# Reload of x split around the turned Wp pieces, and one load of normalised rows moved behind the last turn of q

## The chip, the core and the metric

The kernel runs on one core of one Trainium2 chip. Its engines are TensorE (matmuls, PE in the profile; its weight loads are PEld), VectorE (DVE), ScalarE (ACT), GpSimd (POOL) and SyncE (SP, which here only issues DMAs). Each engine works through its own instructions in their order, and semaphores let one wait for another. DMAs are issued by SP, ScalarE and GpSimd and run on the core's 16 DMA engines; a DMA that the code calls `dma_start_transpose` turns 2-byte blocks on the way. The metric is the device time of one execution in microseconds (us).

## The reference

Forward and backward pass of one transformer block, B=1, S=2048 rows, D=640, H=32 heads of 20, F=1728, all in bfloat16.

```python
h  = x + attn(layernorm(x), wqkv, wo)      # linear attention:
#   q, k, v = heads of x @ wqkv;  phi(t) = where(t > 0, t + 1, exp(t)) + 1e-6
#   kv = phi(k)^T v;  z = sum(phi(k));  o = phi(q) kv / (phi(q) z + 1e-6);  attn = o @ wo
h2 = h + (silu(n @ w1) * (n @ w3)) @ w2    # n = layernorm(h)
# outputs: h2, and the gradients of x, wqkv, wo, w1, w3 and w2 for a given grad_out
```

## The kernel before

The order of all work is written out by hand: within an engine the instructions stand in the order in which the Python code issues them, and tile pools and semaphores are derived from that. Rows of x come in 16 tiles of 128; `x_sb` holds them in on-chip memory, normalised in place. TensorE does nearly all the work and goes through these stages:

- 0 to 73 us: layernorm of x, the k part and a few q tiles (`q_tile`), and the product of phi(k) with the normalised x (`m_part(m, tiles)`, line L430, five blocks m of 128 columns, each over all 16 row tiles). `m_part(4, ...)` is the last reader of the normalised x: it runs in three calls, over tiles 0 to 4, 5 to 10 and 11 to 15. While it runs, finished q tiles are divided by their denominators (`r_row`) and turned into `pqT` by a DMA (`r_T(t)`, L385).
- 73 to 98 us: the remaining q tiles (`q_late`), the folded matrix Wp (`f2_wT(i)`, i from 0 to 4: matmuls L705, copies on ScalarE and VectorE L708, and a turning DMA per 128 columns, L709), and the first attention outputs `f2_half(t, j)` (`f2_at`, matmuls L657; j is the half of 320 columns). They are added to the rows of the raw x, so x has been loaded again into `x_sb` by then: `load_x(a, b)`, L187, loads tiles a to b-1. For tiles 0 to 3 with j=0 and for tile 4 VectorE adds x (L664), for the others of the first eight TensorE does it with an identity matmul (L655). Between them stand single `mlp_ghh(n)` steps (L395, tile `mm`), which read 128 columns each of the turned second weight, `w2T` (`load_w2T(a, b)`, L457); columns 4*128 to 8*128 belong to n = 4 to 7.
- 98 to 340 us: the gated MLP; then to 398 us the gradient of w2, and to 535 us the backward pass through the MLP's layernorm and the attention output (`ghn`, `gr`).
- 535 to 561 us: `q_parts()` (L1219, tile `gwo`), a generator of 20 steps; it makes q's gradient-side products in five blocks m of 128 columns. When a block is done ScalarE copies it to `qp` (L1222), and SP turns it into `QT` (L1226; both are parts of the tile `tri`). `part(n)` runs the next n steps, and the loads of the stage are issued between them: `load_xnT(c)` (L1242) loads and turns 512 normalised rows, `load_wqT(k)` (L1299) loads and turns 640 rows of wqkv.
- 561 to 612 us: four half jobs of the q gradient (`fill(4)`, tile `job`), then `gkvT` (L1388), five blocks whose fourth and fifth read the last block of QT, then small squares, and from 580 us a loop over the 16 row tiles that uses `xnT` (L1441, tile `dkv`, three buffers). In each round VectorE adds `gzb` into `gp` (L1444) and multiplies with `pkb` (L1445), which `load_pk` (L1410) loads by pairs of tiles.
- 612 to 699 us: the gradient of x (`gxn`), and from 699 us the gradients of w1 and w3 (`grad_job`, tile `job`, eight accumulators, 16 matmuls each): ScalarE copies each finished job to a slot of `obs` and issues its stores.

On SP's queue the stretch of the first part of the change reads, in order: r_T(0), r_T(1), a turn of m, r_T(2), `load_w2T(4P, 8P)`, r_T(3), `load_x(0, 6)`, the five Wp pieces, r_T(4), r_T(5). The stretch of the second part reads: turn of QT block 0, `load_xnT(1)`, blocks 1, 2 and 3, `load_xnT(2)`, block 4, `load_xnT(3)`, `load_wqT(0)`, the load of m (`mN`), the store of `dwoT`, four loads of pk.

The DMAs that SP and ScalarE issue take eight semaphores in turn; each waits until the one that last used its semaphore, eight before it, has landed.

Of the kernel before, what the change touches and what calls it, by code (L numbers as in the profile page):

```python
# [9 lines left out]
P = 128  # L10
# [10 lines left out]
ST, DT = S // P, D // P  # L21
# [34 lines left out]
def kernel(  # L56
# [74 lines left out]
    class Stats:  # L131
# [13 lines left out]
        def part(self, src, t, j, mid=None):  # L145
            if j == 0:
                self.st[t] = cp.tile([P, 2, 6], F32, name="st6", bufs=4)
            V.bn_stats(out=self.st[t][:, j, :], in_=src[:, t, j * HD:(j + 1) * HD])
            if j == 0:
                return  # L150
            V.bn_aggr(out=self.mv[:, t, :], in_=self.st.pop(t)[:])
            if mid is not None:
                mid()
            V.tensor_scalar(out=self.ve[:, t:t + 1], in0=self.mv[:, t, 1:2], scalar1=EPS_LN, scalar2=None, op0=ALU.add)
            G.tensor_tensor(out=self.rs[:, t:t + 1], in0=self.ve[:, t:t + 1], in1=mhalf[:, 0:1], op=ALU.pow)
# [30 lines left out]
    def load_x(a, b):  # L186
        dma(out=x_sb[:, a:b, :], in_=xS[:, a:b, :])  # L187
# [86 lines left out]
    def p1_mm(t, n0, between=None, halves=None):  # L274
        acc = p1_acc() if halves is None else None
        for j in range(2):
            p1_half(acc[:, j, 0:HD] if halves is None else halves[j][:, 0:HD], t, n0 + j * HD)
            if j == 0 and between is not None:
                between()
        return acc  # L280
# [9 lines left out]
    def phi(acc, dst, t, parts=None):  # L290

        mq, rq = parts or phi_tiles()
        if parts is None:
            kw = dict(scale=ln1.rs[:, t:t + 1]) if t < RAW else {}
            A.activation(two(mq[:]), acc[:, :, 0:HD], AF.Exp, **kw)
            A.activation(two(rq[:]), acc[:, :, 0:HD], AF.Relu, **kw)

        def rest():
            V.tensor_scalar(out=mq[:], in0=mq[:], scalar1=1.0, scalar2=1e-6, op0=ALU.min, op1=ALU.add)
            V.tensor_tensor(out=dst, in0=mq[:], in1=rq[:], op=ALU.add)  # L300
        held.append(rest)
# [9 lines left out]
    def q_home(t):  # L311
        if t < 4 or 8 <= t < 10:
            pqs[t] = pq6[:, t if t < 4 else t - 4, :]
        elif t < 8:
            pqs[t] = pf.tile([P, D], BF16, name="pql", bufs=4)[:]
        else:
            pqs[t] = pkx[0][:, DT + t - 10, :]
# [3 lines left out]
    def q_tile(t):  # L321
        q_home(t)
        phi(p1_mm(t, 0), pqs[t], t)
# [35 lines left out]
    def r_prod(t):  # L359
        for j in range(2):  # L360
            js = slice(j * HD, (j + 1) * HD)
            if t < 8:
                pr[t, j] = (p1.tile([P, HD], F32, name="pr", bufs=2) if t % 2 else
                            pf.tile([P, HD], F32, name="pr", tag="h2", bufs=2))[:]
            else:
                pr[t, j] = ps.tile([P, 512], F32, name="prp", tag="at", bufs=2)[:, 0:HD]
            (G if t < 8 else V).tensor_tensor(out=pr[t, j], in0=pqs[t][:, js], in1=Zb[:, js], op=ALU.mult)
# [16 lines left out]
    def r_T(t):  # L384
        dmaT(out=pqT[:, :, t * P:(t + 1) * P], in_=pqs[t])  # L385
# [39 lines left out]
    def m_part(m, tiles, js=(0, 1)):  # L425
        if m not in macc:
            macc[m] = [ps.tile([P, 512], F32, name="macc", tag=("m", "tr")[m % 2], bufs=2) for _ in range(2)]
        for t, j in [(t, j) for t in tiles for j in js]:
            n = HD + (m < 2) * j
            T.matmul(macc[m][j][:, 0:n], lhsT=pk_all[:, t, m * P:(m + 1) * P],  # L430
                     rhs=x_ext[:, t, j * HD:j * HD + n], start=(t == 0), stop=(t == ST - 1))
# [12 lines left out]
    def kvT_block(m, acc):  # L444

        a, b = M_H[m]
        n = (b - a) * DH
        for c in range(DT):
            T.matmul(acc[:, 0:n], lhsT=wqkv[:, c, 2 * D + m * P:2 * D + (m + 1) * P],
                     rhs=mT[:, c, a * DH:b * DH], start=(c == 0), stop=(c == DT - 1))  # L450
        masked(bd, acc[:, 0:n], m)
# [4 lines left out]
    def load_w2T(a, b):  # L456
        dmaT(out=w2T[:, :, a:b], in_=B_w2[a:b, :])  # L457
# [116 lines left out]
    def big():  # L574
        return ps.tile([P, 2, 512], F32, name="bigx", tag="big", bufs=2)[:, 0]
# [45 lines left out]
    m_part(3, range(11, ST))  # L621
    m_end(3)
    r_T(2)
    load_w2T(4 * P, 8 * P)
    dmaG(out=m_v[:, 1:4, :], in_=mbs[:, 1:4, :])
    r_head(3)
    r_prod(5)
    m_part(4, range(5))
    q_tile(8)
    kvT_block(1, big())  # L630
    r_row(4)
# [6 lines left out]
        m_part(4, range(11, ST), (j,))  # L638
        m_end(4, (j,))
    ps.release()  # L640
    load_x(0, 6)


    ps = pool("pap", space=PSUM)
# [56 lines left out]
    def f2_wT(i):  # L701

        acc = [ps.tile([P, 512], F32, name="wt", tag=("o2", "at")[i % 2], bufs=2) for _ in range(2)]
        for c, a, b, bank, off, first in SQ:
            T.matmul(acc[bank][:, off:off + (b - a) * DH], lhsT=wo[:, c, i * P:(i + 1) * P],  # L705
                     rhs=bd[:, c, a * DH:b * DH], start=first, stop=True, skip_group_check=True)
        for bank, (a, b) in enumerate(((0, SPLIT_D), (SPLIT_D, H))):
            (A.copy, V.tensor_copy)[bank](out=pkx[0][:, i, a * DH:b * DH], in_=acc[bank][:, 0:(b - a) * DH])  # L708
        dmaT(out=Wp[:, :, i * P:(i + 1) * P], in_=pkx[0][:, i, :])  # L709
# [234 lines left out]
    def kv3():  # L944
# [2 lines left out]

    run((q_late, 10, f2_mT), (q_late, 11, kv3), (phi_rest,),
        (q_late, 12, lambda: (f2_wT(0), f2_wT(1))), (q_late, 13, lambda: (f2_wT(2), f2_wT(3))),
        (f2_wT, 4), (phi_rest,), (q_late, 14), (r_T, 4), (r_head, 5), (r_prod, 7),  # L950
        (q_out, 10, 14), (mlp_ghh, 4),
        (q_late, 15), (w2_room,), (sig_table,), (f2_half, 0, 0), (f2_half, 1, 0), (f2_half, 2, 0), (f2_half, 3, 0), (mlp_ghh, 5),
        (f2_half, 0, 1), (r_store, 4, 5), (f2_half, 1, 1), (f2_hn, 0), (r_store, 5, 6), (f2_half, 2, 1), (f2_hn, 1),
# [42 lines left out]
    for c in range(SC):  # L996
# [9 lines left out]
        for fc in range(FT):  # L1006
# [8 lines left out]
            if c == 0 and fc in (5, 7, 9, 11):  # L1015
                a, b = {5: (0, 3), 7: (3, 6), 9: (6, 10), 11: (10, 13)}[fc]
# [13 lines left out]
            if c == SC - 1 and fc in (1, 2, 5, 6):  # L1030
                i = (1, 2, 5, 6).index(fc)
# [48 lines left out]
    for n in range(len(blk) * DT):  # L1080
        b, m = divmod(n, DT)
# [155 lines left out]
    def load_xnT(c):  # L1237

        if c % 2 == 0:
            both = ba.tile([P, 2, DT, W], BF16, name="xnT", tag="ggb", bufs=2)  # L1240
            xnT[c], xnT[c + 1] = both[:, 0], both[:, 1]
        dmaT(out=xnT[c], in_=xn_d[c * W:(c + 1) * W, :])  # L1242
# [48 lines left out]
    a, b = ST - 1, ST - 2  # L1291
# [20 lines left out]
    load_xnT(1)  # L1312
    part(4)
    part(4)
    load_xnT(2)
    part(20)
    V.reduce_sum(out=gz[:], in_=gz8[:], axis=AX.X)


# [5 lines left out]
    def grad_job(lhs, m, rhs, n, out, q=dma):  # L1325
        for _ in grad_halves(lhs, m, rhs, n, out, q):
            pass
# [107 lines left out]
    for t in range(ST):  # L1435
        c, i = divmod(t, TPC)
# [38 lines left out]
    def load_block(i, a=0, b=NB):  # L1475
        if i < len(blocks):
            f0, f1 = blocks[i]
            if a == 0:
                gb[i] = ex.tile([P, ST, NB], BF16, name="gb", bufs=2)
            b = min(b, f1 - f0)  # L1480
            dmaT(out=gb[i][:, :, a:b], in_=gg_d[f0 + a:f0 + b, :])

    def both_grads(m, f0, f1):

        return [(max(f0, lo) - f0, min(f1, lo + F) - f0, out[:, m, max(f0, lo) - lo:min(f1, lo + F) - lo])
                for lo, out in ((0, out4S), (F, out5S)) if max(f0, lo) < min(f1, lo + F)]
# [57 lines left out]
    def gw2_turn(b):  # L1544
        n = (blk[b][1] + P - 1) // P
        dmaT(out=g_h[:, turned[b]:turned[b] + n, :], in_=gw2T_d[:, b * 512:b * 512 + n * P])

    def gw2_out(b):
        f0, fw = blk[b]
        n, k = fw // P, turned[b]  # L1550
        dma(out=out_6[f0:f0 + n * P, :].rearrange("(k p) d -> p k d", p=P), in_=g_h[:, k:k + n, :])
        if fw % P:
            dma(out=out_6[f0 + n * P:f0 + fw, :], in_=g_h[0:fw % P, k + n, :])

    for i, (f0, f1) in enumerate(blocks):
        n = f1 - f0
        for m in range(DT):
            last = (i, m) == (len(blocks) - 1, DT - 1)
            for a, b in ((0, n - P), (n - P, n)) if last else ((0, n),):
                c = (a + b) // 2  # L1560
                halves = ((a, c), (c, b)) if i * DT + m < 7 else ((a, b),)
                out = [(x + y - a, z + y - a, to) for y, w in halves for x, z, to in both_grads(m, f0 + y, f0 + w)]
                grad_job(hnN, m, lambda t: gb[i][:, t, a:b], b - a, out, A.dma_start)
        load_block(i + 2)
        if 0 < i <= 4:
            gw2_out(i - 1)
        if i < 4:
            gw2_turn(i)
# [36 lines left out]
```

## Time and profile before

| | |
|---|---|
| median of 3 runs | 819.78 us (819.46 to 819.90) |
| the profiled execution | 820.36 us, of which 818.6 us lie between its first and last instruction (its span) |
| TensorE clock granted | 1.000 |
| instructions | 13711 |
| read from and written to HBM | 47.09 MB and 53.43 MB |

Times in the profile count from the first instruction. A line of a timeline gives start, duration, engine, source line, operation, what it writes and reads, shape, how many instructions are merged into it, and in brackets how long the engine was idle before and what ended that. An engine with a q behind its name (SPq) is its sequencer, which issues DMAs; the duration there is that of the issue, and the transfer lands later. A line of waits gives the waiting line, what released it, the total in us, how often, and the longest.

### The profile page before, as it was taken

The numbers are of one execution on the slowest core, as the hardware profiler recorded it, in microseconds if no ns is written. First come the engines' busy times: TensorE is split into PE (matmuls) and PEld (weight loads), VectorE is DVE, ScalarE is ACT, GpSimd is POOL, SyncE is SP. The second block draws the span as 40 slices with busy tenths as digits, with TensorE's granted clock in tenths as the row PEclk, the third lists the DMA queues.
The fourth block names the chain that finished last, engine by engine and source line by source line (L and its number), as shares of the span: only waits on it lengthen the run. The fifth ranks groups of instructions, "written<-read, shape, count | busy, mean of one in ns | idle before, by whom it ended". The sixth has DMA issues, their size and how long they took to land.

```text
span 818.6 us, 13711 instructions
## 1 busy us (share of the span) xinstructions
PE 811.6 (99%) x5261; PEld 501.6 (61%) x5292; DVE 452.7 (55%) x973; ACT 324.8 (40%) x609; POOL 131.7 (16%) x198
## 2 busy tenths in 40 slices
PE   9999999999999999999999999999999999999998
PEld 6777544555555555754577777777777777544444
DVE  7859997998898566300057777772781544200000
ACT  7856688665565666011112212222212334211111
POOL 2243333323222212100001111110220000000000
PEclk9999999999999999999999999999999999999999
DMA  9899899696485556999877877269994888979991
GB/s 262 207 242 277 206 276 302 207 244 174 128 209 158 169 168 168 239 254 243 233 178 181 218 194 193 58 111 181 269 217 93 179 193 153 249 175 235 221 239 37
DMA packets 335889, 162.46 MB, mean 198 GB/s; under 512 B 252560, under 2 KB 329072, under 8 KB 335824
## 3 DMA queue, kind: packets, MB, share of 16 engines
q1 hardware_dynamic: 291920, 120.68, 63.8%
q0 software_dynamic: 7328, 24.48, 8.9%
q10 hardware_dynamic: 36576, 16.42, 8.2%
q8 instruction: 41, 0.67, 0.3%
q14 instruction: 24, 0.20, 0.1%
HBM read 47.09 MB, written 53.43 MB: 123 GB/s over the span
## 4 chain that ended last, share of the span: by engine, by line
PE 96%; DMA 1%; ACT 1%; DVE 1%; issue 0%; SPq 0%; POOL 0%; DVEq 0%
PE mm L395 20%; PE job L1335 19%; PE ghn L1131 14%; PE gxn L1504 8%; PE gw L1086 7%; PE big L268 4%; PE o L913 4%; PE o L859 3%; PE gwo L1219 3%; PE macc L430 3%; PE gr L1188 3%; PE dkv L1441 3%; PE at L657 2%; DMA wqkv<-in_A_wqkv_dram 1%; PE dkv L1369 1%; DMA tri<-tri 1%
## 5 line engine op out<-in xcount | busy, mean ns | idle before, releaser
L1335 PE MATMUL job<-gb,hnN 128*128 128x496 bf16 (+3 forms) x576 | 116.8, 366 | 0.0
L1131 PEld LDWEIGHTS <-ggb 128*128 128x128 bf16 x864 | 84.5, 98 | 33.0
L395 PE MATMUL mm<-pqT,w 128*128 128x512 bf16 x396 | 93.2, 379 | 0.5
L1335 PEld LDWEIGHTS <-hnN 128*128 128x128 bf16 x576 | 55.8, 98 | 61.0
L395 PEld LDWEIGHTS <-w 128*128 128x128 bf16 x540 | 52.6, 98 | 62.9 <-issue 0.6
L1339 ACT CAST obs<-job 128x496 bf16<-128x496 f32 (+4 forms) x56 | 28.5, 510 | 123.6 <-PE job L1335 123.6
L1131 PE MATMUL ghn<-w13a,ggb 128*128 128x320 bf16 x448 | 63.5, 299 | 0.0
L1146 DVE SCALAR_TENSOR_TENSOR wb<-gs,hnb 128x640 f32<-128x640 bf16 x16 | 13.2, 825 | 88.1 <-ACT gs L1143 88.1
L1131 PE MATMUL ghn<-w13b,ggb 128*128 128x320 bf16 x416 | 61.4, 299 | 0.0
L395 PE MATMUL mm<-g2T,w2T 128*128 128x512 bf16 x228 | 58.8, 379 | 0.6
L1086 PE MATMUL gw<-hb,g 128*128 128x512 bf16 (+2 forms) x316 | 58.4, 345 | 0.2
L1086 PEld LDWEIGHTS <-g 128*128 128x128 bf16 x320 | 31.3, 98 | 27.0
L420 ACT CAST ghh<-mm 128x512 bf16<-128x512 f32 x48 | 28.2, 588 | 48.2 <-PE mm L395 41.4
L1196 POOL TENSOR_TENSOR sz<-Zb,g_h 128x640 f32<-128x640 bf16 x16 | 20.2, 1262 | 163.7 <-DVE g_h L1197 163.7
L796 ACT ACTIVATE sig<-mm 128x512 bf16<-128x512 f32 x56 | 33.7, 602 | 25.0 <-PE mm L395 21.6
L1143 ACT ACTIVATE gs<-ghn 128x640 bf16<-128x640 f32 x16 | 11.3, 705 | 76.0 <-PE ghn L1131 76.0
L395 PEld LDWEIGHTS <-w2T 128*128 128x128 bf16 x260 | 25.4, 98 | 23.4
L268 PEld LDWEIGHTS <-pqT 128*128 128x128 bf16 x320 | 30.7, 98 | 13.5 <-ACT pqT L260 0.9
L268 PE MATMUL big<-wqkv,pqT 128*128 128x320 bf16 x250 | 38.4, 299 | 0.2
L1335 PEld LDWEIGHTS <-g 128*128 128x128 bf16 x320 | 31.0, 98 | 11.5
L832 DVE TENSOR_TENSOR gate<-gate,sig 128x1024 bf16<-128x1024 bf16 x28 | 19.3, 689 | 33.9 <-ACT gate L807 31.1
L1091 ACT CAST gw2o<-gw 128x512 bf16<-128x512 f32 (+2 forms) x20 | 10.4, 519 | 66.6 <-PE gw L1086 25.3
(217 smaller groups left out, 1391.2 us busy)
## 6 DMA issues: line engine op xcount, KB each, us to landing
hh_d<-hhT SPq DMA_DIRECT2D x24, 256.0 KB, 2.8
gg_d<-gate POOLq DMA_DIRECT2D x24, 256.0 KB, 4.4
gg_d<-ghh POOLq DMA_DIRECT2D x24, 256.0 KB, 4.1
ggb<-gg_d SPq DMA_DIRECT2D x6, 896.0 KB, 5.3
ggb<-gg_d ACTq DMA_DIRECT2D x6, 832.0 KB, 5.7
ggb<-gg_d SPq DMA_DIRECT2D x2, 1728.0 KB, 13.9
pk_d<-pk_all SPq DMA_DIRECT2D x4, 640.0 KB, 5.4
g<-in_grad_out_dram SPq DMA_DIRECT2D x4, 640.0 KB, 5.7
```

Source lines behind the costliest of these rows:

```text
L268: T.matmul(acc, lhsT=pqT[:, c, t * P:(t + 1) * P], rhs=wqkv[:, c, n0:n0 + HD], start=(c == 0), stop=(c == DT - 1))
L395: T.matmul(acc[:], lhsT=w[:, c, fc * P:(fc + 1) * P], rhs=rhs[:, c, :], start=(c == 0), stop=(c == DT - 1))
L420: A.copy(out=ghh[n // 2][:, n % 2, :], in_=acc[:])
L430: T.matmul(macc[m][j][:, 0:n], lhsT=pk_all[:, t, m * P:(m + 1) * P], rhs=x_ext[:, t, j * HD:j * HD + n], start=(t == 0), stop=(t == ST - 1))
L796: A.activation(sig[:, i, :], gp[:], AF.Sigmoid)
L859: T.matmul(accs[i, j][:, 0:HD], lhsT=hhT[c][:, fc, i * P:(i + 1) * P], rhs=w2[:, fc, j * HD:(j + 1) * HD], start=(first and fc == 0), stop ...
L913: T.matmul(o2["ps"][:, 0:HD], lhsT=hhT[c][:, fc, i * P:(i + 1) * P], rhs=w2[:, fc, j * HD:(j + 1) * HD], start=(fc == 0), stop=(fc == FT - 1))
L1086: T.matmul(acc[:, 0:fw], lhsT=g2[:, t, m * P:(m + 1) * P], rhs=hb[b][:, t, 0:fw], start=(t == 0), stop=(t == ST - 1))
L1131: T.matmul(acc[:, j, 0:HD], lhsT=ggb[t // 2][:, k, lo:lo + P], rhs=rhs[:, j * HD:(j + 1) * HD], start=(k == 0), stop=(k == NG - 1))
L1335: T.matmul(acc[:, 0:n], lhsT=lhs[:, t, m * P:(m + 1) * P], rhs=rhs(t), start=(t == 0), stop=(t == ST - 1))
L1339: A.copy(out=ob, in_=acc[:, 0:n])
L1504: T.matmul(acc[:, j, 0:HD], lhsT=g, rhs=wqT[:, k, j * HD:(j + 1) * HD], start=(k == 0), stop=(k == 14))
```

## The change

Three moves, and no arithmetic is altered.

1. The reload of x, one DMA of six tiles after the last `m_part`, becomes two: `load_x(0, 4)` right after the first call of `m_part(4, ...)`, and `load_x(4, 6)` in the next stage, behind the five Wp pieces and ahead of r_T(4). `load_w2T(4P, 8P)`, which stood ahead of r_T(3), becomes two DMAs of 256 columns behind `load_x(0, 4)`.
2. `load_xnT(2)` moves from ahead of the last three steps of `q_parts` to behind them, and so behind the turn of QT's block 4.
3. In the last stage the first five jobs, instead of the first seven, have their store split into halves.

```diff
     m_end(3)
     r_T(2)
-    load_w2T(4 * P, 8 * P)
     dmaG(out=m_v[:, 1:4, :], in_=mbs[:, 1:4, :])
     r_head(3)
     r_prod(5)
     m_part(4, range(5))
+    load_x(0, 4)
+    load_w2T(4 * P, 6 * P)
+    load_w2T(6 * P, 8 * P)
     q_tile(8)
...
     ps.release()
-    load_x(0, 6)
...
         (q_late, 12, lambda: (f2_wT(0), f2_wT(1))), (q_late, 13, lambda: (f2_wT(2), f2_wT(3))),
-        (f2_wT, 4), (phi_rest,), (q_late, 14), (r_T, 4), (r_head, 5), (r_prod, 7),
+        (f2_wT, 4), (load_x, 4, 6), (phi_rest,), (q_late, 14), (r_T, 4), (r_head, 5), (r_prod, 7),
...
     load_xnT(1)
     part(4)
     part(4)
+    part(20)
     load_xnT(2)
-    part(20)
...
-                halves = ((a, c), (c, b)) if i * DT + m < 7 else ((a, b),)
+                halves = ((a, c), (c, b)) if i * DT + m < 5 else ((a, b),)
```

On SP's queue the first stretch now reads: r_T(2), r_T(3), `load_x(0, 4)`, the two halves of w2, the five Wp pieces, `load_x(4, 6)`, r_T(4), r_T(5). In the second, `load_xnT(2)` and block 4 have changed places. TensorE, VectorE and GpSimd have the same instructions in the same order as before; ScalarE issues two DMAs fewer.

## The prediction

> **What bounds the kernel now.** I read the busy table first, then TensorE's waits, then, around each wait, TensorE's and the DMA issuer's timelines, the chain and the landing times.
>
> ```profile
> PE 811.6 (99%) x5261; PEld 501.6 (61%) x5292; DVE 452.7 (55%) x973; ACT 324.8 (40%) x609; POOL 131.7 (16%) x198
> ```
>
> TensorE is the bound from end to end, so a change pays only where TensorE waits. Its waits are all here (engine, line, releaser, us):
>
> ```profile
> PE warm L468 <- DVE zero L125: 1.1, 1, 1.1
> PE k L268 <- DMA wqkv<-in_A_wqkv_dram: 0.6, 2, 0.4
> PE gkvT L1388 <- DMA tri<-tri: 0.5, 1, 0.5
> PE at L657 <- DVE rden L378: 0.2, 1, 0.2
> ```
>
> The first two belong to the start, which the change leaves alone; the last two stand where it acts. A row understates them: a 320-column matmul lasts 0.30, yet 54 of the ghn ones take 7.33 in the chain, 0.136 each, so a row ends some 0.16 after the next matmul could have begun.
>
> TensorE's timeline at the `at` wait:
>
> ```profile
> 84.63 0.71 PE L268 MATMUL mm<-wqkv,pqT 128*128 128x320 bf16 x4
> 85.57 0.30 PE L657 MATMUL at<-Wp,pqT 128*128 128x320 bf16 x1 [0.24 <-DVE rden L378]
> ```
>
> So the true loss is 0.24 + 0.16 = 0.40: TensorE could have begun at 85.17. The releaser named, an unrelated reciprocal, ended at 85.35; an `at` half reads Wp columns 0 to 319, the first three turned pieces. SP's timeline there:
>
> ```profile
> 72.77 3.19 SPq L457 DMA_TRANSPOSE w2T<-in_B_w_dram  x1
> 76.06 1.22 SPq L385 DMA_TRANSPOSE pqT<-hx  x1
> 77.38 1.40 SPq L187 DMA_DIRECT2D x_sb<-in_A_x_dram  x1
> 79.66 6.59 SPq L709 DMA_TRANSPOSE Wp<-pkx  x5
> 86.69 1.92 SPq L385 DMA_TRANSPOSE pqT<-pql  x1
> ```
>
> The five pieces are issued at 79.66, 80.96, 82.39, 83.73 and 85.05, and the DMA view gives 4.5, 3.8, 3.1, 2.7 and 2.6 from issue to landing. The third lands at 85.49, and TensorE goes on 0.08 later. The landings shorten as the load of six rows ahead (960 KB, issued 77.38, landing 6.1 later) clears: the pieces stood behind it.
>
> The chain at the other wait, and SP's timeline around it:
>
> ```profile
> 560.73 1.48 PE job L1335 x11
> 562.21 4.25 DMA tri<-tri
> 566.45 0.05 issue
> 566.50 0.78 PE gkvT L1388 x10
> ```
>
> ```profile
> 554.86 3.87 SPq L1226 DMA_TRANSPOSE tri<-tri  x3
> 558.77 3.34 SPq L1242 DMA_TRANSPOSE xnT<-xn_d  x1
> 562.21 1.22 SPq L1226 DMA_TRANSPOSE tri<-tri  x1
> 563.48 3.57 SPq L1242 DMA_TRANSPOSE xnT<-xn_d  x1
> 567.09 3.97 SPq L1299 DMA_TRANSPOSE wqT<-in_A_wqkv_dram  x1
> ...
> 572.66 3.34 SPq L1410 DMA_DIRECT2D pkb<-pk_d  x4
> ```
>
> q's last block is copied by ScalarE at 560.76 for 0.69, ready at 561.45, but SP is issuing `load_xnT(2)` until 562.11 and its data lie ahead, so the turn lands 4.25 after issue where its predecessors take 2.6 to 2.7. The row's 0.47 idle plus 0.16 makes 0.63.
>
> **The change, part by part.** Part A, the rows of x. SP issues r_T(3) right behind r_T(2): its rows are scaled on VectorE by 72.37 (71.40 + 0.97), so 72.77 to 74.0. `load_x(0, 4)` writes rows whose last reader is m_part(4, range(5)), done on TensorE by 67.0, so SP does not stop there; its issue lies between the 0.57 of two rows (at 104.43) and the 1.40 of six, say 1.0. The w2 halves take 1.35 each (the 256-column piece at 97.90) to 1.6 (half of 3.19). SP is free by 77.7 to 78.3; the first Wp piece goes at 79.66 as before, since VectorE finishes its copy at 79.58. Issue times stay, and the third piece, at 82.39, lands at 85.0 to 85.1 if it takes the 2.6 to 2.7 of the undisturbed ones: TensorE goes on at 85.17. Gain 0.40; the other end is 0, if the w2 halves (640 KB, now directly ahead) delay the pieces as x did. I take 0.40: the halves are issued three to four us earlier than that x load relative to the third piece, and 320 KB of x have left the queue.
>
> What moved back: the first w2 half is first used by the matmuls at 82.73. Issued at about 75.0, it lands at 78.9 with the 3.9 of the piece at 97.90, at 81.8 with the 6.8 of the old load; both in time. The second is needed at 93.5. Rows 0 to 3 come earlier, for VectorE's add at 86.45.
>
> `load_x(4, 6)` now stands between the fifth Wp piece and r_T(4). It delays r_T(4)'s issue by 0.57 and puts 320 KB before it. That turn landed at 91.0 (86.69 + 4.3) and TensorE uses it at 92.63, now 92.23: cover 1.2. Ends: 0.57 (issue only: no wait) and 0.57 + 3.4 (the whole landing of the two-row load at 104.43, in series: 95.0, a wait of 2.7). The data rate that the 79.5 to 83.0 window shows, 290 GB/s, makes 1.1 for 320 KB; with the issue hidden behind the data I take 1.0 to 1.1, landing 92.1, no wait. Rows 4 and 5 themselves are wanted at 95.06, nearly 9 us after issue. Behind them SP used to wait 2.98 for the first normalised block (90.14 to 93.12), which absorbs the 0.57.
>
> Part B, `load_xnT(2)` behind the last turn of q. SP issues the turn at 561.5; with nothing before it, it lands 2.6 to 2.7 later, 564.15. gkvT's fourth block can begin when its third is through, 565.87. Gain 0.63. Price: SP's row of loads moves. It had finished the wqT load at 571.06; now turn 1.22, xnT(2) 2.74 (the one at 552.03, likewise right behind a turn) to 3.34, xnT(3) 2.74 to 3.57, wqT 3.4 (2.74 for 640 rows instead of 512) to 3.97: 571.7 to 573.7, later by 0.6 to 2.6. mN, dwoT_d and pkb follow. xnT(2) is first used at 596, and mN, which landed at 577.0, at 585.3: both have room. The tight one is pkb's first pair: issued 572.66, landing 8.8 later at 581.5, and VectorE:
>
> ```profile
> 581.76 0.83 DVE L1444 TENSOR_TENSOR gp<-dkv,gzb 128x640 f32<-128x640 f32 x1 [1.77 <-PE dkv L1441]
> 582.62 0.82 DVE L1445 SCALAR_TENSOR_TENSOR g_k<-pkb,gp 128x640 bf16<-128x640 bf16 x1
> ```
>
> Measured in old times less 0.63, VectorE wants it at 582.0. If late, the second gp waits behind on VectorE, and with it the dkv tile that TensorE's fourth block (585.62, now 584.99) reuses: from landing L the tile is free at L + 0.86 + 0.06 + 0.83 + 0.05, so TensorE waits when L passes 583.2. L is 582.1 to 584.1. In old SP times the DMAs stood idle between 564.4 and 566.5 in part, which the closer row fills, so I take 1.4 late, 582.9: no wait. Ends for part B: 0.63 to -0.3.
>
> Part C, fewer halves: two DMA issues of 0.34 to 0.44 less on ScalarE near 717 to 724, two whole stores instead of four halves. TensorE ran the last 576 matmuls with no wait, on eight accumulators. Price 0; were a store 3 us later, its obs slot is not rewritten for six jobs of 3.3 us. With two DMAs more in part A and two fewer here, the eight semaphores that SP's and ScalarE's DMAs take in turn fall as before from the sixth stored job on.
>
> Sum: -0.40 - 0.63 + 0 = -1.03. The profiled execution took 820.36, 818.6 of it span and 1.7 around it, 0.58 above the median of 819.78; it would become 819.33, the median 818.75.
>
> **Rivals.** (1) pkb too late: L at its late end, 584.1, costs 0.9: part B -0.3, total 819.7; half-way 819.2. For it: pkb's landing has 8.8 us of queue before it. Against: 1.4 late would do no harm.
>
> (2) Block 4 of pqT too late: POOL's 640 KB store of pq_d is issued at 85.62 and lands at 90.3, so three transfers meet. The half-way wait is 0.7 to 1.3: 819.4 to 820.0.
>
> (3) Slower: transfers of one queue pay their start and end one after another, so that two more DMAs cost two more such times. A turned tile lands 2.6 after issue, and its 160 KB at 290 GB/s are 0.6 of it: 2.0 each. The extra w2 half puts 2.0 ahead of the Wp pieces, the two rows taken out give back 1.1: the third piece lands at 86.4, the wait grows by 0.9 and part A loses that instead of gaining; r_T(4) adds up to 1.5. With part B: 819.78 + 0.9 + 1.5 - 0.63 = 821.5. It decides when the third piece lands after 85.5. Against it: five pieces issued 1.3 apart, each taking 2.6 or more, land 0.6 to 1.3 apart, so those times overlap. The Trainium skill, "DMA: Bandwidth & Descriptors", sections "Anatomy of one DMA — SWDGE (gpsimd) path" and "Rules for kernel authors", speaks against the split: about 2.0 us fixed for each DMA, so many small transfers should be joined into one large. The trace agrees on the 2 us of a lone turn, not on their adding up.
>
> (4) The moves do nothing (Wp's pieces late for another reason, the turn of q no faster): 819.8. Against it are the undisturbed 2.6 landings.
>
> **How the numbers follow.** Forecast 0.58, its own range 818.5 to 819.1 (0.25 either way); rival 1 0.16; rival 2 0.11; rival 3 0.07; rival 4 0.05; 0.03 for something else. A gain over 1.03 has no wait to come from. The range 818.4 to 820.0 holds the forecast and rivals 1, 2 and 4 (0.90, and about 0.85 after the ends of each). For this kernel 0.2%, 1.6 us, is taken as what a measurement tells from no change: faster would be below 818.14, slower above 821.42. The forecast and most rivals lie between: faster 0.05, same 0.86, slower 0.09 (rival 3 and the worst of 2).
>
> **What would show it.** In TensorE's waits after: no `at` wait near 85.5, no gkvT wait near 566. Wp's third piece lands under 2.7 after issue; the last turn of q is issued before `load_xnT(2)` and lands within 2.7. Wrong if a new TensorE wait stands at the `at` matmuls of tile 4 (92) or the ghh matmuls at 82.7 (part A), or at dkv near 585 with VectorE waiting on pkb (part B).

## The result, and the profile after

The changed kernel took 822.47 us (median of 18 runs, 820.97 to 827.85), the kernel before 819.79 (18 runs, 819.21 to 821.54): a ratio of 1.0036 with a 95% interval of 1.0024 to 1.0047. It is slower, by 2.7 us; 818.75 was predicted, and the time lies outside the range.

Two executions of the changed kernel were profiled, one of 824.2 us (span 822.3) and one of 822.3 us (span 820.4). The second stands at the median and is the better picture; the first shows what a longer wait brings with it. The busy table of the first, and then TensorE's waits (line, releaser, total, times, longest):

```profile
PE 813.6 (99%) x5261; PEld 501.2 (61%) x5292; DVE 452.7 (55%) x973; ACT 324.7 (39%) x609; POOL 131.9 (16%) x198
```

```profile
PE at L658 <- DMA Wp<-pkx: 2.0, 1, 2.0
PE warm L468 <- DVE zero L125: 1.1, 1, 1.1
PE dkv L1442 <- DVE gp L1445: 0.5, 1, 0.5
PE k L268 <- DMA wqkv<-in_A_wqkv_dram: 0.2, 1, 0.2
```

The same view of the second execution:

```profile
PE at L658 <- DMA Wp<-pkx: 1.1, 2, 0.6
PE dkv L1442 <- DVE gp L1445: 1.0, 1, 1.0
```

Line numbers are one higher than before. The gkvT wait is gone, as forecast. The `at` wait is not: in the first execution a new one of 2.0 stands at the fifth Wp piece, in the second there are two, at the third piece and at the fifth. And a new wait stands at dkv. With 0.16 added to each row, as in the prediction, the losses are (us):

| where | before | after, 824.2 | after, 822.3 |
|---|---|---|---|
| `at`, third piece | 0.40 | 0.31 | 0.70 |
| `at`, fifth piece | 0 | 2.20 | 0.72 |
| half clock behind it | 0 | 1.74 | 0 |
| gkvT, last block of q | 0.64 | 0 | 0 |
| dkv, tile of pk | 0 | 0.64 | 1.20 |
| sum less the sum before | | +3.85 | +1.58 |
| span less the span before | | +3.7 | +1.8 |

(The third piece's 0.31 in the first execution is the gap between two matmul starts, 0.44, less the 0.13 that one takes; it has no row of its own.) The table accounts for both spans to 0.2. SP's timeline of the first execution, and then of the second (start, duration, line, operation, how many merged):

```profile
74.32 0.53 SPq L187 DMA_DIRECT2D x_sb<-in_A_x_dram  x1
74.90 4.25 SPq L457 DMA_TRANSPOSE w2T<-in_B_w_dram  x2
79.63 7.52 SPq L710 DMA_TRANSPOSE Wp<-pkx  x5
87.21 1.57 SPq L187 DMA_DIRECT2D x_sb<-in_A_x_dram  x1
```

```profile
75.01 4.99 SPq L457 DMA_TRANSPOSE w2T<-in_B_w_dram  x2
80.18 8.39 SPq L710 DMA_TRANSPOSE Wp<-pkx  x5
88.62 0.58 SPq L187 DMA_DIRECT2D x_sb<-in_A_x_dram  x1
```

The five pieces take 7.52 us of SP's queue from 79.63 and 8.39 from 80.18, where the kernel before needed 6.59 from 79.66. The w2 halves take 4.25 and 4.99: the first 1.33 and 1.34, the second 2.87 and 3.60. The fifth piece is issued at 85.74 and 86.15 instead of 85.05. TensorE's timeline at the fifth piece, first in the kernel before (one line), then in the second execution (two):

```profile
89.50 0.84 PE L657 MATMUL at<-Wp,pqT 128*128 128x320 bf16 x5
```

```profile
89.68 0.30 PE L656 MATMUL at<-x_sb,ident 128*128 128x320 bf16 x1
90.53 0.85 PE L658 MATMUL at<-Wp,pqT 128*128 128x320 bf16 x5 [0.56 <-DMA Wp<-pkx]
```

The fifth piece landed at 87.64 in the kernel before; in the second execution it lands at 90.49, and at 91.55 in the first, where a row of busy times by stretches shows what followed (stretch, its length, busy time and count of PE, PEld, DVE, ACT, POOL, then the granted clock, the DMA share and GB/s):

```profile
91.60:95.00 3.40, 3.40 (x13) 1.92 (x14) 0.86 (x3) 0.71 (x2) 0.41 (x1) 0.51 0.50 118
```

TensorE's clock is half for 3.4 us: thirteen 320-column matmuls go at 0.267 each instead of 0.133, which is the 1.74 of the table.

At dkv, VectorE's timeline of the first execution, then TensorE's:

```profile
584.78 0.82 DVE L1445 TENSOR_TENSOR gp<-dkv,gzb 128x640 f32<-128x640 f32 x1 [1.77 <-PE dkv L1442]
587.48 0.82 DVE L1446 SCALAR_TENSOR_TENSOR g_k<-pkb,gp 128x640 bf16<-128x640 bf16 x1 [1.88 <-DMA pkb<-pk_d]
588.41 0.82 DVE L1445 TENSOR_TENSOR gp<-dkv,gzb 128x640 f32<-128x640 f32 x1
```

```profile
589.29 1.52 PE L1442 MATMUL dkv<-small,xnT 128*128 128x320 bf16 x10 [0.48 <-DVE gp L1445]
```

VectorE's multiplication by `pkb` stands 1.88 for the first pair of pk, the second `gp` waits behind it, and TensorE's fourth block waits for the dkv tile: rival 1 step by step.

### The profile page after: what moved, and what is told of

Same layout as the page of the kernel before. It is cut to its first block, busy times and chain, and to the rows that moved or that the text cites. A ratio compares the mean times of both kernels' runs of the same rounds, so it can differ in the third digit from the quotient of the medians.

```text
span 822.3 us, 13711 instructions
## 1 busy us (share of the span) xinstructions
PE 813.6 (99%) x5261; PEld 501.2 (61%) x5292; DVE 452.7 (55%) x973; ACT 324.7 (39%) x609; POOL 131.9 (16%) x198
## 4 chain that ended last, share of the span: by engine, by line
PE 95%; DMA 2%; DVE 1%; ACT 1%; issue 0%; SPq 0%; POOL 0%; ACTq 0%; DVEq 0%
PE mm L395 20%; PE job L1336 19%; PE ghn L1132 14%; PE gxn L1505 8%; PE gw L1087 7%; PE big L268 4%; PE o L914 4%; PE o L860 3%; PE gwo L1220 3%; PE macc L430 3%; PE gr L1189 3%; PE at L658 3%; PE dkv L1442 2%; PE mm L268 1%; DMA pkb<-pk_d 1%; DMA Wp<-pkx 1%
```

## The experiments

All ratios are to the kernel before on the same chip, with 95% intervals. One execution of each kernel was profiled, and a second one of three of them.

**The parts by themselves.** First the rows of x with the w2 halves, alone; then the load of normalised rows, alone.

> The first part alone: x reloaded in two pieces and the w2 load split and moved, nothing else changed. Theory S (the w2 halves ahead of the Wp pieces slow their issue, the fifth piece slides under GpSimd's store of pq_d and lands some 4 us later): all of the loss is here, an at wait of about 2 us near 89 to 91 and a time of 822 to 823, now and then more when the TensorE clock is halved behind the wait. Rival (the loss is spread over both parts): about half of it here, 821.

> The second part alone: one load of normalised rows behind the last turn of q. Theory P (the 0.63 won at gkvT is given back at dkv, where VectorE waits for pkb): 819.8 within 0.2, no gkvT wait, a dkv wait of 0.5 to 0.7. If pkb's lateness in the changed kernel came from the first part, the gain stands: 819.15 and no dkv wait. Rival (the second part loses by itself): over 820.2.

Rows alone: 821.46 (820.49 to 824.57), ratio 1.0021 (1.0007 to 1.0034). Normalised rows alone: 820.51 (819.99 to 821.74), 1.0008 (0.9999 to 1.0016). The second one's waits and its SP timeline:

```profile
PE dkv L1441 <- DVE gp L1444: 1.0, 1, 1.0
```

```profile
561.30 1.20 SPq L1226 DMA_TRANSPOSE tri<-tri  x1
562.54 6.90 SPq L1242 DMA_TRANSPOSE xnT<-xn_d  x2
569.49 3.65 SPq L1299 DMA_TRANSPOSE wqT<-in_A_wqkv_dram  x1
```

The turn lands 2.60 after issue and the gkvT wait is gone; pk's first pair is issued at 574.50 and lands at 584.06, and TensorE loses 1.17 at dkv (the gap between two starts less what the first matmul takes). The last part, fewer halves, was run alone as well:

```diff
-                halves = ((a, c), (c, b)) if i * DT + m < 7 else ((a, b),)
+                halves = ((a, c), (c, b)) if i * DT + m < 5 else ((a, b),)
```

> The kernel before with only the last part of the change: two gradient blocks near 720 stored whole instead of in halves. The prediction's price 0: 819.6 to 820.2, no wait of TensorE after 700. A rival: a whole store lands later and holds its output slot, 820.3 or more with a wait of TensorE in the last 100 us.

820.18 (819.45 to 823.08), 1.0002 (0.9992 to 1.0012): nothing, as priced. Its profiled execution was the longest of the twelve and does show waits near 700 (0.3 at `gxn`, 0.8 at a gradient job), but both are for loads and stand some 15 us ahead of the edited stores; 1.4 of its 2.7 us of extra span stand at 75 to 86. So most of the loss is in the first part, and the second part pays at dkv what it gains at gkvT, or more.

**Is it GpSimd's store?** In the first execution of the changed kernel, by the trace's packet records, the fifth piece's packets run from 86.91 to 90.89, in between those of the 640 KB store of pq_d (87.16 to 90.75). The store was moved to SP, behind r_T(5), in the changed kernel and in the kernel before:

```diff
     def q_out(a, b):
-        dmaG(out=pq_v[:, a:b, :], in_=pkx[0][:, DT + a - 10:DT + b - 10, :])
+        dma(out=pq_v[:, a:b, :], in_=pkx[0][:, DT + a - 10:DT + b - 10, :])
```

> The changed kernel with one more edit: the store of q tiles 10 to 13 (pq_d) is issued by SP behind r_T(5) instead of by GpSimd at 85.6, so that it cannot run beside the fifth Wp piece. Theory S: the at wait is gone, the fifth piece lands about 2.6 to 3 after issue, the time falls to 819.4 to 820.0. Rival X (the two rows of x behind the piece hold it) and rival W (the w2 halves hold it): the wait of about 2 us stays, 822 to 822.5.

> Control for the run above: the kernel before with the same store moved to SP behind r_T(5). All theories: the time of before within 0.3 (819.5 to 820.1), the 0.24 at wait at 85.5 still there, since the third Wp piece still stands behind six rows of x.

The changed kernel with it: 823.01 (821.42 to 825.49), 1.0038 (1.0027 to 1.0049), no better. The kernel before with it: 819.94 (819.80 to 820.60), 0.9996 (0.9988 to 1.0005), the same time, but all twelve runs within 0.8. In the profiled execution of the first the fifth piece lands at 88.12 and the `at` matmuls wait for nothing, so the store was what held the piece. But the span is still 2.4 above that of the second (820.6 and 818.2): 1.56 of it at dkv, 0.36 more at the transposes of the third normalised tile, 0.43 at the `mm` matmuls behind them. The expectation that the store is the whole loss fell.

**SP's stop.** In every profiled execution with the first part as the change has it SP stands idle for 0.50 or 0.51 ahead of the fifth piece, with the piece's data ready for over a us; in the kernel before it stands 0.44 behind that piece. Counting SP's DMAs gives the pattern: in all twenty profiled executions of this study the gap of 0.43 to 0.52 stands ahead of SP's 53rd DMA, whatever that is, and those right before and behind it have 0.05 to 0.13. The change puts one more DMA ahead of the pieces, so the fifth one becomes the 53rd. The expectations from here on name three theories. N: one more DMA ahead of the pieces moves the stop to before the fifth. W: the w2 data directly ahead of the pieces make them late. X: rows 4 and 5 ahead of r_T(4) make r_T(4), r_T(5), the store of r and so the third normalised tile late. To test N alone, the kernel before got its x load split in place:

```diff
-    load_x(0, 6)
+    load_x(0, 4)
+    load_x(4, 6)
```

> The kernel before with nothing moved: its load of six rows of x is only split in two, rows 0 to 3 and rows 4 and 5, in the old place. Theory N: one more DMA ahead of the pieces, so SP stops ahead of the fifth piece, which is issued 0.3 to 0.6 later than before (85.4 to 85.7) and lands at 88.3 or later; 820.4 to 821.5. Theories W and X: nothing changes, 819.5 to 820.2.

The gap moved as expected (fifth piece issued at 85.33, landing at 88.89), and this edit alone, which moves nothing, took 821.79 (820.23 to 824.12), 1.0020 (1.0010 to 1.0030). Yet its profiled execution, its fastest, has no wait for the piece. A second profiled execution of it:

> The split-load kernel again, for a second profiled execution: the first one was its fastest (820.2 of 820.2 to 824.1) and showed the fifth Wp piece late but no wait for it. If the extra DMA costs through that piece, an execution near 822 shows TensorE waiting 0.5 to 2.5 at the at matmuls near 90 for it; if not, the wait stands elsewhere: at the third normalised tile near 95, at mT near 76, or in the start.

819.90, again an undisturbed execution: the piece, issued at 85.43, lands at 88.82, its packets run from 86.60 to 87.58 and the store's only from 87.50, and TensorE has no `at` wait; it would have begun to wait at 89.20. The same with the store on SP:

> The kernel before with its load of six rows split in two in place (as in the split-load run, which cost 1.7 us) and the store of pq_d issued by SP behind r_T(5) instead of by GpSimd. If what the extra DMA costs is the fifth Wp piece meeting the store: that piece, still issued 0.4 to 0.7 late, lands within 2.8 of its issue, and the time is 819.8 to 820.6 with no run above 821.2, as with the store moved and the load unsplit. If the extra DMA costs by another way: median 821 or more, single runs to 823.

820.88 (820.18 to 824.68), 1.0014 (1.0002 to 1.0025): 0.6 above the kernel before on its chip at the median, where the split load with GpSimd's store was 1.7 above. But the two intervals overlap, so that part of the cost goes through the store is likely and not shown. Four runs of twelve lie above 821.2, against the expectation; of the kernel before six of 29 do on that chip. Which wait the dearer executions of the split load contain was not seen in a trace and stays open: the extra DMA's cost is shown in time, its way is not.

**The place of w2.** Two kernels leave the count of DMAs ahead of the pieces as it was: one with the first part but w2 unsplit in the new place, one with nothing but w2 moved, unsplit, between the load of six rows and the pieces (the edit below).

```diff
     r_T(2)
-    load_w2T(4 * P, 8 * P)
...
     load_x(0, 6)
+    load_w2T(4 * P, 8 * P)
```

> The rows-of-x part of the change with the w2 load in its new place but unsplit: one DMA fewer ahead of the Wp pieces, the same bytes. Theory N: SP's 0.45 us stop is back behind the fifth piece, which lands by 87.8; 819.5 to 820.3. Theory W (640 KB of w2 directly ahead of the pieces): 821 to 822, the pieces landing over 3 us after issue. Theory X: 821 to 822 with the pieces in time.

> The kernel before with only the w2 load moved, unsplit, from ahead of r_T(3) to between the load of six rows and the Wp pieces; no split, the same number of DMAs, rows 4 and 5 where they were. Theory W: SP issues w2 until 80 or later, so the first piece goes 0.4 or more late, the pieces land later than before and the third one's wait grows to 0.8 or more; 820.8 to 823. If the place of w2 costs nothing without the extra DMA: 819.6 to 820.4.

The first took 823.00 (821.42 to 825.28), 1.0033 (1.0021 to 1.0046); the second 821.90 (821.37 to 822.39), 1.0018 (1.0009 to 1.0027), with even its shortest run 1.1 above the median of the kernel before on that chip (820.25). SP's timeline of the second, and TensorE's:

```profile
74.20 0.53 SPq L187 DMA_DIRECT2D x_sb<-in_A_x_dram  x1
74.78 5.57 SPq L457 DMA_TRANSPOSE w2T<-in_B_w_dram  x1
80.53 7.36 SPq L709 DMA_TRANSPOSE Wp<-pkx  x5
```

```profile
83.68 1.25 PE L395 MATMUL mm<-g2T,w2T 128*128 128x512 bf16 x4 [0.84 <-DMA w2T<-in_B_w_dram]
...
91.60 0.58 PE L657 MATMUL at<-Wp,pqT 128*128 128x320 bf16 x3 [1.03 <-DMA Wp<-pkx]
```

The same load that took 3.19 of SP's queue ahead of r_T(3) takes 5.57 behind the x load. SP is free at 80.35, the first piece goes 0.9 late, the fifth at 86.41 with the stop behind it as in the kernel before; its packets come behind the store's (87.18 to 89.58) and it lands at 91.55. So w2's place is a cause by itself, shown in time and trace. Not all of this carries over to the changed kernel: the wait for w2 itself (0.84 and 0.16) is not there, since the first half lands by 82.39.

**Rows 4 and 5 ahead of r_T(4).** w2 back in its old place, unsplit, and only the x load split around the pieces; and the reverse, the first part with rows 4 and 5 moved behind r_T(5):

```diff
-        (f2_wT, 4), (load_x, 4, 6), (phi_rest,), (q_late, 14), (r_T, 4), (r_head, 5), (r_prod, 7),
+        (f2_wT, 4), (phi_rest,), (q_late, 14), (r_T, 4), (r_head, 5), (load_x, 4, 6), (r_prod, 7),
```

> The kernel before with the load of rows 0 to 3 as in the change and rows 4 and 5 behind the Wp pieces, but the w2 load unsplit in its old place ahead of r_T(3). Theory N (one more DMA on SP ahead of the Wp pieces moves a 0.45 us stop of SP from behind the fifth piece to before it, and the piece meets GpSimd's store): as many DMAs stand ahead of the pieces as before, so the stop stays behind the fifth piece, which is issued by 85.1 and lands by 87.8; 819.5 to 820.2. Theory W (the w2 data directly ahead of the pieces): also 819.5 to 820.2. Theory X (rows 4 and 5 ahead of r_T(4) make r_T(4), r_T(5), the store of r and so the third normalised tile late): 821 to 822.

> The rows-of-x part of the change with w2's halves where the change has them, but rows 4 and 5 behind r_T(5). Theory N alone is left (one more DMA ahead of the pieces, the fifth issued 0.4 to 0.7 late): if it is the larger part, 820.8 to 821.6 with single runs up to 824, as the part itself; if theory X is, 819.5 to 820.3.

The first took 821.15 (820.53 to 822.85), 1.0010 (1.0001 to 1.0019). All pieces are in time (fifth at 87.46), and its only new wait is

```profile
PE trh L768 <- DVE hn L161: 1.2, 1, 1.2
```

r_T(4) and r_T(5) land at 92.15 and 92.67 instead of 91.00 and 91.66, GpSimd's first store of r lands 4.28 after issue instead of 2.13, at 96.30, and VectorE writes the third normalised tile, whose buffer that store reads, at 96.38. The second took 822.66 (822.36 to 824.06, six runs), 1.0029 (1.0018 to 1.0040): moving rows 4 and 5 away does not help where the pieces are late. In its trace, and in that of the kernel with w2 unsplit, the turned m had already come late near 75 (a wait of 0.7 and 1.3 at `kv`), w2's issue ended at 81.5 and 81.1, and the pieces were late in full. That early wait also stood in the execution with only the stores changed; it comes and goes from one execution to the next, and 0.9 and 1.5 of what these two profiled executions lose belong to it.

With neither cause (w2 in place, as many DMAs ahead of the pieces, rows 4 and 5 behind r_T(5)):

> The kernel before with its load of six rows split: rows 0 to 3 in the old place, rows 4 and 5 behind r_T(5), so neither theory's cause is there: as many DMAs ahead of the Wp pieces as before (theory N), and nothing new ahead of r_T(4) and r_T(5) (theory X). If the two are the whole loss: the fifth piece lands by 87.8, r_T(4) and r_T(5) by 91.8, no wait at the transposes of the third normalised tile above 0.3, 819.2 to 820.2 with the third piece's wait of 0.4 gone. If something else of the move costs: 820.5 or more.

820.59 (819.87 to 822.96), 1.0004 (0.9996 to 1.0013): the loss is gone, but there is no gain.

**pk's landing, and a version that keeps both ideas.** The load of wqT was moved behind the four pk loads, first with the second part alone, then with that and the last kernel above, then with the second part and the store on SP:

```diff
     load_xnT(3)
-    load_wqT(0)
...
         load_pk(n)
+    load_wqT(0)
```

> The kernel before with the load of normalised rows behind the last turned block of q, and the load of wqT moved from ahead of the four pk loads to behind them. If the loss of that part comes from pk's tile being late, it now lands by 582 (old times), TensorE's wait at dkv goes below 0.2, and the time is 819.2 to 819.8. If another transfer of that row is what is late, the wait stays or moves: 820.3 to 821.

> Both ideas of the change without what the runs found to cost: rows 0 to 3 in the old place and rows 4 and 5 behind r_T(5); the load of normalised rows behind the last turned block of q, with the load of wqT behind the four pk loads. If the causes are found: 818.7 to 819.6, below the kernel before by 0.2 to 1.0. If not: 820.3 or more.

> A candidate: the normalised rows behind the last turned block of q, wqT behind the pk loads, and the store of pq_d on SP behind r_T(5). The waits at gkvT and dkv are gone and the store is off the Wp pieces: 819.2 to 819.8, no run above 821. If the moved loads collide with others in some executions: 820.2 or more.

820.61 (819.29 to 822.71), 1.0005 (0.9995 to 1.0015); 820.87 (820.02 to 829.24), 1.0033 (1.0010 to 1.0056); 822.02 (820.37 to 830.98), 1.0029 (1.0008 to 1.0051). In the first one's profile (span 817.8) neither the gkvT nor the dkv wait is left, so pk's landing was the cause of the latter. But the time is not better, and the other two have executions of 823.8 to 831. The profiled execution of the last one (823.63) has neither of the two waits. Apart from 1.1 at the very start, which the kernel before has too, its longest are:

```profile
PE k L268 <- DMA wqkv<-in_A_wqkv_dram: 1.3, 2, 0.9
PE tr L258 <- DVE x_sb L161: 1.2, 1, 1.2
```

Both stand before 22 us: of the 3.3 us that its span is longer than the kernel before's, 2.7 are lost before 40 us, ahead of every edit. So an execution can be long without any of the edits, and the medians of a dozen runs carry that too. A second profiled execution of the middle one was also long:

> The version meant to keep both ideas of the change, again, for a second profiled execution: 5 of its 12 executions took 823.8 to 829.2. If the load of wqT behind the pk loads is what is late in those, TensorE waits for a transfer between 585 and 640; if rows 4 and 5 are, between 90 and 100.

824.18. Its waits and SP's timeline:

```profile
PE dkv L1441 <- DVE gp L1444: 2.3, 1, 2.3
...
PE gxn L1504 <- DMA bd<-g_k: 0.8, 1, 0.8
```

```profile
572.59 3.21 SPq L1409 DMA_DIRECT2D pkb<-pk_d  x4
575.84 8.87 SPq L1299 DMA_TRANSPOSE wqT<-in_A_wqkv_dram  x1
584.81 6.81 SPq L1427 DMA_TRANSPOSE wqT<-small  x5
591.67 8.26 SPq L1299 DMA_TRANSPOSE wqT<-in_A_wqkv_dram  x1
599.98 11.51 SPq L1463 DMA_TRANSPOSE pkT<-pk_d  x1
```

In its new place wqT holds SP for 8.87, where it took 3.97, and all behind it slides. A later pair of pk, loaded by GpSimd, lands 14.98 after issue instead of 5.91 in the kernel before; TensorE loses 2.5 near 609 and 1.0 near 629. In the same kernel's other profiled execution (820.14) wqT held SP as long, 9.13, and that pair landed 11.32 after issue, in time; what tips an execution over is not shown. No version tried beats the kernel before. The second profiled execution of the changed kernel itself, used above, had this expectation:

> The changed kernel itself, for a second profiled execution. If the fifth Wp piece meets the store in every execution and only the length of the meeting varies, the piece is again issued 0.4 or more after the fourth one's end and lands over 3 us after issue, with or without a wait of TensorE; dkv waits 0.6 to 1.6 for pk's tile in any case.

It came out that way: the fifth piece 0.50 after the fourth one's end, landing 4.34 after issue, here behind nearly the whole of the store (87.01 to 89.38, the piece's packets from 88.89), and a dkv loss of 1.20.

## Why the prediction was wrong

**Part A, "Issue times stay"** is the step that failed, and with it the estimate that the w2 halves take 1.35 to 1.6 each and leave SP free by 77.7 to 78.3. The second half took 2.87 and 3.60, SP was free at 79.15 and 80.00, the first piece's issue took 1.65 or began 0.5 late, and SP's stop moved to before the fifth piece. That one went at 85.74 and 86.15, not at 85.05. The 1.35 came from a lone load of 256 columns and the 1.6 from halving the old load; that the load of x now stood directly ahead of them was not weighed, and directly behind x the whole load takes 4.82 and 5.57.

**Part A, the third piece only.** The prediction followed the piece that TensorE waited for and not the one next in line. The fifth landed at 87.64 and was needed at 89.50, a cover of 1.86 that looks large and was never worked out. It has a cliff in it: the piece's packets ended at 87.18 and the store's began at 87.16. A piece 0.7 to 1.1 later interleaves with the store or comes behind it, and lands 2.8 to 3.9 later. The store was weighed, in rival 2, against r_T(4) alone. The Trainium skill, "DMA: Bandwidth & Descriptors", section "Queues, rings and completion order", says that each DMA engine takes turns between queues packet by packet; the trace of the 824.2 execution agrees, with the piece's 256-byte packets spread from 86.91 to 90.89 between the store's of 5120 bytes.

**Part A, rows 4 and 5.** With these alone r_T(4) landed at 92.15, where 92.1 was forecast, and nothing waited for it. What was missed stands behind it: the store of r on GpSimd's queue lands at 96.30, and the third normalised tile needs its buffer. In both profiled executions of the changed kernel TensorE was late already, and that wait did not come. Rival 2 looked at r_T(4) too, and did not come.

**What followed the wait.** No term stood for the clock. The wait of 2.2 cost 1.74 more at half clock; the granted clock was below 0.999 in 4 of 18 runs (0.996 to 0.998), the profiled one among them.

**Part A, the gain of 0.40.** It was read off one execution. The wait for the third piece is 0.40 there, but the kernel before with the store on SP and that with only the normalised rows moved show none, with the piece issued within 0.2 of where it was. It is a wait of some executions, and 0.40 was its price in one of them.

**Part B, gain** 0.63: the wait went as worked out, with the turn landing 2.57 to 2.60 after issue (2.6 to 2.7 forecast). But it too stood only in some executions: in the rows alone, the split load and the kernel before with its store on SP there is no gkvT wait to remove.

**Part B, "1.4 late, 582.9: no wait"** is the mis-sized term. Less what TensorE had lost or won up to gkvT, so that it compares with the prediction's times, L was 583.6 and 584.2 in the changed kernel and 584.25 with the part alone; there the issue was 2.0 late, within the 0.6 to 2.6 given, and the landing took 9.57 instead of 8.83. The threshold of 583.2 held: L past it by 0.4, 1.0 and 1.05 cost 0.64, 1.20 and 1.17. Rival 1, given 0.16, was the case, and was taken as harmless since the middle of the range was.

**Part C** was right at 0, by its own run.

**Rival 3** had the sign and nearly the size (821.5), by another mechanism: the first four pieces land 0.6 to 1.3 apart as before, so fixed times do not add up. The 2.0 us fixed for each DMA in its last argument belongs, by the section title that it names, to DMAs issued by GpSimd; these loads are SP's. Its threshold, the third piece past 85.5, was crossed in one execution of two (85.75 and 85.33).

The causes do not add: by the medians w2's place alone costs 1.7, one more DMA 1.7, rows 4 and 5 1.0, and all three together 1.8. A likely reason, argued and not shown, is that each makes the same few transfers late, so that TensorE waits once for several of them. How much of the part's loss belongs to each is not settled.

## What to carry to other kernels

When a DMA is moved past others, work out the cover of every transfer behind it, not just of the one that is waited for now, and look for what its packets would meet if it came half a us later: here a cover of 1.86 had a 640 KB store right behind the piece's packets. An issue time of a turning load holds only for the place where it was read. A wait of half a us in one execution is no sure gain: two or three executions of the unchanged kernel tell whether it is there each time.

## What the runs showed of the hardware

- SP stands still for 0.43 to 0.52 us ahead of its 53rd DMA, in twenty profiled executions of seventeen kernels, whichever transfer that is. An 8 KB packet of a queue that the profile calls instruction begins 0.6 to 2.3 us behind the end of that gap in all twenty; whether the two belong together is not shown. So the number of DMAs, not only their bytes, decides where a short stop falls.
- How long the issue of a turning load takes depends on its place: the same 640 KB of w2 took 2.76 to 3.6 in its old place, and 4.82 and 5.57 behind the load of x; wqT took 3.97 in its old place and 8.49 to 9.13 behind the loads of pk.
- A wait of 2.2 us brought 3.4 us of half clock. The Trainium skill, "TensorE: Matmul & The Clock Gate", section "Part 1: The HAM clock gate (the "warmup" mystery)", gives a free-running window of 3413 ns and idleness of a window as the condition; the length of the slow stretch agrees, the condition does not: here 2.2 us were enough. In the 824.18 execution above, a wait of 2.5 left the granted clock at 1.00 from 580 to 640. The records of the granted clock tell the two apart. In the seventeen profiled executions that have them, the stretch at full clock lasts a whole multiple of 3.413 us (25 times and 213 times in the 824.2 execution, 240 times in the 824.18 one). On that grid the first wait lies within one stretch, 88.25 to 91.67, in which TensorE stood idle for 2.04 by the trace's rows, and the next stretch is at half; the second wait is divided at 609.16, and its larger share is 1.94. From one case on each side, how much idle time in a stretch it takes is not settled.
